# Block attention and a gated feed-forward layer in one kernel: signs of eight weight tiles, one scaling and a run of zero products move to other places

## The chip, the cores and the metric

The kernel runs on one core of one Trainium2 chip. The metric is device time in microseconds (us). Three runs of the kernel before took 1049.8, 1050.09 and 1050.73 us (median 1050.09).

## The reference, cut to what matters

```
scores = 0.125 * q @ k.T            # 8 batches, 8 heads, 576 positions, head size 64
scores = where(block_i >= block_j, scores, -1e9)      # blocks of 64 positions
attn   = exp(scores - rowmax);  attn /= rowsum + 1e-9
x = (attn @ v), heads side by side  # 4608 tokens x 512
h = x @ w_in                        # 512 x 2048, 64-bit floats
g = h * sigmoid(h)
out = g @ w_out                     # 2048 x 512, 64-bit floats
```

The two weight matrices arrive as 64-bit floats and are turned into 32-bit floats on the chip. Every product of the feed-forward layer and of the late attention is done with each 32-bit operand cut into a high part (a rounded copy, `fp32r`) and a low part (the rest).

## The kernel before, in words

The feed-forward layer works on 18 blocks of 256 tokens, each in 8 steps `d` over the 2048 inner columns (256 per step): `ffn1` (line 599, four 128x256 pieces in three products each, for two halves), then `silu` (L606), `g_hi` (L612), `g_lo` (L617) and, two steps later, `ffn2` (L629). One `ffn` in the order is half a step of either.

The tokens of the feed-forward blocks come from three kinds of attention. `First` (`a` and `b`) is the first block of 64 positions for all batches, in two groups; `a` yields block 0 of the feed-forward layer and `b` block 1. `Second` (`c0` to `c3`) is the second block of 64 positions. `Unit` (`u0` to `u63`) is one head of one batch for the other 448 positions. For `a`, `b` and `c` the steps are: `load` and `load_v` (DMA), `scores` (TensorE, L505 or L557), `max` and `sub` (VectorE, L433 and L436), `exp` (ScalarE, L439), `sum` (VectorE, L444 to L447), `norm` (the scaling by 1/sum, L450; on VectorE for `a` and `b`, on GpSimd for `c`), `turn` (transposes on TensorE, L457), `back` (ScalarE, L460), `pv` (TensorE, L519 or L575), `hi` (ScalarE, L524 or L580) and `lo` (VectorE, L528 or L583).

The weights come in 32 tiles `w0` to `w31` of 128x512 64-bit words: `w0`, `w1` belong to step 0 of `ffn1`, `w2`, `w3` to its step 1, `w4`, `w5` to step 0 of `ffn2`, `w6`, `w7` to step 2 of `ffn1`, and so on in turn. A tile is loaded (L187 or L190), the upper word scaled on ScalarE (`rebias`, L200), put together in three bit steps on VectorE (`bits:0`, `bits:1`, `bits:2`, L208, L212, L216; the first shifts and masks, the second adds the sign, the third adds the bits of the lower word), and cut into the high part (`hi`, ScalarE, L224) and the low part (`lo`, GpSimd, L227). Between `bits:0` and `bits:2` the half-made tile stands in a bank of PSUM.

The order of everything up to the 17th `Unit` is written out by hand in the string `ORDER`; a loop over the rest follows. Each engine runs its own instructions in that order and waits only for data and for free buffers. Loads all go through the queue of SyncE, in order. The buffers of `a`'s and `b`'s query and key tiles are used again by `w2` to `w5`, those of `b`'s scores (`T`) by `w7`.

Before the first real product TensorE multiplies 18 pairs of 64-column zero tiles (L415).

Of the kernel before, what the change touches and what calls it, by code (L numbers as in the profile page):

```python
# [55 lines left out]
a.lo:0 a.hi:1 b.pv w4.bits:0 w3.hi a.lo:1 w3.lo c0.load w4.bits:1 ffn w4.bits:2 b.hi:0 w7.load w2.lo b.hi:1 w5.bits:0 w8.load
w4.hi ffn w5.bits:1 w6.rebias w4.lo b.lo:0 ffn w5.bits:2 b.lo:1 w9.load w6.bits:0 c0.scores:0 silu w6.bits:1 g_hi ffn w6.bits:2
w7.rebias g_lo c0.max:0 w10.load w8.rebias ffn w7.bits:0 c0.load_v w5.hi w7.bits:1 silu w5.lo ffn c0.sub:0 w6.hi w7.bits:2 g_hi
w6.lo w8.bits:0 c0.scores:1 w9.rebias w11.load w7.hi w8.bits:1 ffn w10.rebias w8.bits:2 w7.lo w9.bits:0 w8.hi w12.load ffn g_lo
w9.bits:1 w9.bits:2 ffn w8.lo c0.max:1 w9.hi w13.load w10.bits:0 w11.rebias ffn w9.lo c0.sub:1 silu w10.bits:1 g_hi w10.bits:2 ffn  # L60
g_lo w11.bits:0 w14.load c0.exp w11.bits:1 ffn w11.bits:2 w12.rebias c0.sum w10.hi ffn w15.load w13.rebias w10.lo w12.bits:0 ffn
c0.norm w12.bits:1 silu w11.hi w12.bits:2 ffn w14.rebias w13.bits:0 w16.load w12.hi w11.lo w13.bits:1 c0.turn:0 c1.load g_hi ffn
w13.bits:2 c0.back:0 w12.lo w15.rebias w14.bits:0 w17.load c0.turn:1 w14.bits:1 g_lo ffn c0.back:1 w14.bits:2 w13.hi w15.bits:0
w16.rebias c0.pv w18.load w13.lo silu w15.bits:1 ffn w15.bits:2 c0.hi w16.bits:0 w14.hi w19.load g_hi ffn c0.lo w14.lo w17.rebias
w16.bits:1 w16.bits:2 c1.scores:0 g_lo w17.bits:0 w20.load ffn w17.bits:1 silu c1.max:0 w15.hi ffn c1.sub:0 w18.rebias w15.lo
w17.bits:2 g_hi w16.hi c1.scores:1 w18.bits:0 w21.load w17.hi g_lo w18.bits:1 w19.rebias ffn w18.bits:2 w16.lo w19.bits:0 ffn
w18.hi w22.load c1.max:1 w17.lo w20.rebias w19.bits:1 ffn silu w19.bits:2 w18.lo w20.bits:0 w19.hi w23.load ffn w20.bits:1
w21.rebias w19.lo g_hi c1.sub:1 ffn w20.bits:2 g_lo w21.bits:0 w24.load ffn w21.bits:1 c1.exp w21.bits:2 w20.hi ffn c1.sum
w22.rebias w25.load w20.lo w23.rebias c1.load_v ffn w22.bits:0 c2.load c1.norm w22.bits:1 silu ffn w22.bits:2 w24.rebias w21.hi
w23.bits:0 w26.load c1.turn:0 w23.bits:1 w21.lo ffn c1.back:0 w23.bits:2 g_hi w24.bits:0 w22.hi c1.turn:1 w27.load ffn w24.bits:1  # L70
w22.lo c1.back:1 w25.rebias w24.bits:2 w23.hi c1.pv g_lo w25.bits:0 w28.load w25.bits:1 w26.rebias ffn w23.lo c2.load_v c1.hi
w25.bits:2 w26.bits:0 ffn w29.load c1.lo w27.rebias w24.hi w26.bits:1 c2.scores:0 w25.hi w26.bits:2 w24.lo silu ffn w27.bits:0
w26.hi w30.load w25.lo w27.bits:1 g_hi w28.rebias ffn w27.bits:2 g_lo w29.rebias w28.bits:0 w31.load w27.hi ffn w28.bits:1 w26.lo
w28.bits:2 ffn w29.bits:0 w27.lo w30.rebias w29.bits:1 ffn w29.bits:2 w31.rebias w30.bits:0 silu ffn w30.bits:1 g_hi w30.bits:2
ffn g_lo w31.bits:0 c3.load c2.max:0 ffn c2.sub:0 silu w31.bits:1 w29.hi g_hi c2.scores:1 w31.bits:2 w28.hi ffn w28.lo c2.max:1
u0.load c2.sub:1 c3.scores:0 g_lo ffn mask c3.max:0 c2.exp c3.sub:0 w29.lo w31.hi c3.scores:1 c2.sum w30.hi w31.lo c3.load_v ffn
c3.max:1 c2.norm c3.sub:1 ffn c3.exp ffn w30.lo c3.sum c2.turn:0 silu ffn c2.back:0 c3.norm u0.split_hi c2.turn:1 ffn c2.back:1
g_hi c3.turn:0 g_lo c2.pv c3.back:0 c3.turn:1 u0.split_lo u0.load_v ffn c3.back:1 silu c3.pv g_hi ffn g_lo u1.load c3.hi c2.hi
c3.lo ffn c2.lo output silu u0.scores g_hi u0.v_hi g_lo ffn u0.max u1.split_hi ffn u1.split_lo u0.max2 ffn silu output ffn u0.v_lo
u2.load u0.sub ffn u1.load_v g_hi store g_lo u1.scores store u0.exp:0 ffn u1.max u2.split_hi u0.exp:1 ffn u2.split_lo u0.exp:2  # L80
u0.p_hi:0 u1.max2 ffn u0.p_hi:1 ffn u0.p_lo:0 u3.load silu u1.sub g_hi u0.p_lo:1 ffn u0.p_hi:2 u0.sums g_lo u2.scores u0.p_lo:2
silu ffn u2.max u3.split_hi u0.pv u3.split_lo u2.max2 u1.exp:0 ffn u1.exp:1 u1.exp:2 ffn u1.p_hi:0 u4.load g_hi u2.sub u1.p_lo:0
u1.p_hi:1 ffn u1.v_hi u1.p_lo:1 u0.lower u1.sums u1.p_hi:2 ffn g_lo u3.scores u0.fold u1.v_lo u2.exp:0 u1.sums2 u1.p_lo:2 ffn
u2.load_v u4.split_hi output ffn u3.max u4.split_lo output u2.exp:1 u1.pv u2.exp:2 u3.max2 ffn silu u5.load g_hi ffn u2.p_hi:0
g_lo u3.sub u1.lower u2.p_hi:1 ffn u2.p_lo:0 silu u1.fold u4.scores u2.p_lo:1 u2.sums g_hi u2.p_hi:2 u2.v_hi ffn u2.p_lo:2 u4.max
ffn u2.v_lo u3.exp:0 g_lo u1.mult u3.exp:1 ffn u3.load_v u5.split_hi u4.max2 u2.pv u3.exp:2 u5.split_lo ffn silu u4.sub u1.x_hi
ffn u2.lower u6.load u1.x_lo u3.p_hi:0 u3.sums ffn u3.p_hi:1 u3.p_hi:2 u3.p_lo:0 u3.v_hi u5.scores g_hi u2.fold u3.p_lo:1 u3.sums2
ffn g_lo u6.split_hi ffn u3.v_lo u5.max silu u3.p_lo:2 u4.load_v ffn u4.exp:0 u5.max2 u6.split_lo u4.exp:1 u3.pv g_hi u4.exp:2 ffn
u4.p_hi:0 u5.sub u3.lower g_lo u7.load u4.v_hi ffn u4.p_hi:1 u4.p_lo:0 u3.fold store u6.scores u4.sums u4.p_lo:1 silu ffn
u4.p_hi:2 u4.v_lo u6.max u7.split_hi ffn u4.p_lo:2 u5.load_v u3.mult ffn u7.split_lo u5.exp:0 u6.max2 u5.exp:1 u4.pv g_hi u5.exp:2  # L90
ffn g_lo u8.load u5.v_hi u6.sub u3.x_hi ffn store u4.lower u3.x_lo u5.p_hi:0 u5.sums ffn u5.p_lo:0 silu u7.scores u5.v_lo u4.fold
u5.p_hi:1 u5.p_hi:2 u5.sums2 u5.p_lo:1 u6.load_v ffn u5.p_lo:2 u6.exp:0 ffn u7.max u8.split_hi g_hi u5.pv u8.split_lo u6.exp:1
u6.exp:2 u7.max2 ffn u6.p_hi:0 u5.lower u6.v_hi ffn g_lo u9.load u6.p_hi:1 u7.sub ffn u6.p_lo:0 u5.fold u6.v_lo u8.scores silu
u6.sums u6.p_lo:1 g_hi u7.load_v u6.p_hi:2 ffn u9.split_hi g_lo u8.max ffn u6.p_lo:2 silu u5.mult ffn u9.split_lo u8.max2 u7.exp:0
u6.pv u7.exp:1 g_hi u7.exp:2 ffn g_lo u7.p_hi:0 u10.load u8.sub u5.x_hi ffn u6.lower u5.x_lo u7.p_hi:1 u7.sums u7.p_hi:2 ffn
# [710 lines left out]
```

## Time and profile before

| what | value |
|---|---|
| time of the profiled execution | 1050.03 us |
| its span, first to last instruction | 1048.3 us |
| median of three runs | 1050.09 us |
| TensorE busy | 1027.9 us, 98% |
| VectorE busy | 767.1 us, 73% |
| ScalarE busy | 750.5 us, 72% |
| GpSimd busy | 741.4 us, 71% |

The page names the engines PE (TensorE), DVE (VectorE), ACT (ScalarE), POOL (GpSimd) and SP (SyncE). The shares are means over a span that has a start, a stretch in which weights are made, a long steady stretch and an end with only the feed-forward layer; what one stretch waits for is read from its own rows. A record of the profile for a 32-bit float product is half of one, so 18 zero products have 36 records.

### The profile page before, as it was taken

What the parts mean: (1) busy time and instruction counts of PE and PEld (TensorE: products, weight loads), DVE (VectorE), ACT (ScalarE), POOL (GpSimd) and SP (SyncE); (2) the same over time, 40 slices, a digit from 0 to 9 for tenths busy, and PEclk for the clock granted to TensorE, in tenths of its full rate; (3) what the DMA queues carried; (4) which work ended last, traced back from release to release, by engine and by line L of the source; (5) the groups of instructions that cost most, each with busy time, mean ns of one, the idle gap of its engine ahead of it and who ended that gap; (6) DMA issues with size and microseconds to landing.
All of it is one profiled execution on the core that took longest, in us unless ns stands there. A gap on an engine that the chain in (4) does not pass through costs nothing.

```text
span 1048.3 us, 19893 instructions
## 1 busy us (share of the span) xinstructions
PE 1027.9 (98%) x6996; PEld 931.2 (89%) x6996; DVE 767.1 (73%) x2238; ACT 750.5 (72%) x1195; POOL 741.4 (71%) x721
## 2 busy tenths in 40 slices
PE   5999999999999999999999999999999999999998
PEld 4888898888899999999999999998999999989987
DVE  7998499999968888888888887888888888700000
ACT  4876578898987778787878787878788877722222
POOL 1676679888886878787878787878787878622221
PEclk6999999999999999999999999999999999999999
DMA  6777223223223222222222223222222222000000
GB/s 245 248 236 247 58 73 84 70 74 79 65 53 91 54 53 74 54 73 54 74 54 74 59 61 81 56 78 53 73 54 74 54 73 53 18 11 21 1 21 21
DMA packets 35043, 79.93 MB, mean 76 GB/s; under 512 B 4736, under 2 KB 12928, under 8 KB 34944
## 3 DMA queue, kind: packets, MB, share of 16 engines
q1 hardware_dynamic: 34944, 78.66, 26.8%
q8 instruction: 56, 0.92, 0.4%
...
## 4 chain that ended last, share of the span: by engine, by line
PE 82%; DVE 7%; ACT 4%; POOL 3%; issue 2%; DMA 2%; SPq 0%; DVEq 0%; ACTq 0%; POOLq 0%
PE o L629 33%; PE h L599 33%; PE S L289 7%; PE U L368 7%; DVE wm L216 1%; DVE Dx L233 1%; DVE S L212 1%; DMA qkraw<-in_qk_dram 1%; DVE S L208 1%; DVE Mx L233 1%; POOL pl L344 1%; DMA wst<-in_moe_w_in_dram 1%; ACT p L330 1%; PE S L629 1%; ACT g L606 0%
## 5 line engine op out<-in xcount | busy, mean ns | idle before, releaser
L599 PE MATMUL h<-x,wi 128*128 128x256 f32 x3456 | 440.6, 281 | 0.3 <-POOL x L405 0.3
L599 PEld LDWEIGHTS h<-x,wi 128*128 128x128 f32 x3456 | 429.9, 188 | 11.8 <-issue 0.5
L629 PE MATMUL o<-wo,g 128*128 128x512 f32 x1680 | 424.7, 398 | 0.0
L629 PEld LDWEIGHTS o<-wo,g 128*128 128x128 f32 x1680 | 305.8, 188 | 62.6 <-issue 0.3
L344 POOL TENSOR_TENSOR pl<-p,ph 128x448 fp32r<-128x448 f32 (+1 forms) x192 | 226.0, 1201 | 95.2 <-ACT ph L336 95.2
L617 POOL TENSOR_TENSOR g<-g,g 128x512 fp32r<-128x512 f32 x144 | 186.3, 1294 | 122.1 <-ACT g L612 117.1
L233 DVE TRANSPOSE_TENSOR_REDUCE Mx<-S 64x4 f32<-64x128 f32 (+4 forms) x384 | 135.6, 405 | 99.2 <-PE S L289 98.8
L606 ACT ACTIVATE g<-h 128x512 f32<-128x512 f32 x144 | 86.1, 598 | 124.6 <-POOL g L617 75.3
L612 ACT CAST g<-g 128x512 fp32r<-128x512 f32 x144 | 89.2, 619 | 60.8 <-PE o L629 59.0
L233 DVE TRANSPOSE_TENSOR_REDUCE Dx<-p 128x14 f32<-128x448 f32 (+3 forms) x320 | 122.8, 446 | 0.2
L330 ACT ACTIVATE p<-T 128x512 f32<-128x512 f32 (+1 forms) x192 | 105.6, 604 | 12.5 <-POOL ph L346 11.8
L336 ACT CAST ph<-p 128x512 fp32r<-128x512 f32 (+1 forms) x192 | 104.5, 595 | 0.3 <-PE U L368 0.2
L265 POOL TENSOR_TENSOR qh<-qkraw,qh 64x576 fp32r<-64x576 f32 x64 | 91.5, 1430 | 15.3 <-ACT qh L261 10.7
L289 PE MATMUL S<-qh 128*128 128x448 f32 (+3 forms) x320 | 91.1, 298 | 0.0
L606 ACT ACT_TABLE_LOAD x67 | 86.0, 1283 | 1.2
L289 PE MATMUL S<-ql,qh 128*128 128x448 f32 (+3 forms) x320 | 84.0, 307 | 0.0
L330 ACT ACT_TABLE_LOAD x63 | 80.8, 1283 | 1.5
L267 POOL TENSOR_TENSOR ql<-qkraw,qh 128x448 fp32r<-128x448 f32 x64 | 74.1, 1158 | 5.0
L368 PE MATMUL U<-ph,vc 128*128 128x448 f32 (+3 forms) x320 | 74.4, 297 | 1.8 <-DVE xu L384 1.3
L321 DVE TENSOR_TENSOR T<-S,MR 128x256 f32<-128x256 f32 (+2 forms) x192 | 73.1, 407 | 0.0
L261 ACT CAST qh<-qkraw 128x1024 fp32r<-128x1024 f32 x64 | 66.9, 1045 | 6.7 <-DMA qkraw<-in_qk_dram 5.4
L276 POOL TENSOR_TENSOR vc<-vraw,vc 128x320 fp32r<-128x320 f32 x64 | 56.6, 884 | 13.9 <-ACT vc L273 13.4
...
## 6 DMA issues: line engine op xcount, KB each, us to landing
qkraw<-in_qk_dram SPq DMA_DIRECT2D x128, 256.0 KB, 4.0
...
```

What stands on the lines that cost most here:

```text
L233: nc.vector.tensor_reduce(out=out, in_=in_, axis=AX.X, op=op, apply_transpose=True)
L265: nc.gpsimd.tensor_tensor(out=u.qh[64:, NQ:], in0=u.raw[64:, NQ:], in1=u.qh[64:, NQ:], op=ALU.subtract)
L289: nc.tensor.matmul(u.ps(c, w, m), u.kk[:, j * P : j * P + m], qq[:, q0 : q0 + w], start=i == 0, stop=i == 1)
L330: nc.scalar.activation(u.p[:, c:e], T[:, c:e], AF.Exp, scale=SCALE)
L336: nc.scalar.copy(u.ph[:, c:e], u.p[:, c:e])
L344: nc.gpsimd.tensor_tensor(out=u.pl[:, c:e], in0=u.p[:, c:e], in1=u.ph[:, c:e], op=ALU.subtract)
L368: nc.tensor.matmul(U[:m, q0 : q0 + w], u.vc[:, j, :m], (u.ph, u.pl)[pp][:, c : c + w], start=n == 0, stop=n == 8)
L599: nc.tensor.matmul(h[:, f, :], wi[wt][:, c, w], x[:, xt, :], start=n == 0, stop=n == 3 * CT - 1)
L606: nc.scalar.activation(g, hs.pop((blk, d)), AF.Silu)
L612: nc.scalar.copy(g2[:, 0], g)
L617: nc.gpsimd.tensor_tensor(out=g2[:, 1], in0=g, in1=g2[:, 0], op=ALU.subtract)
L629: nc.tensor.matmul(o, g2[:, gt, f, tk], wo[wt][:, 2 * d + f, :], start=d == 0 and n == 0, stop=d == NSTEP - 1 and n == 5,)
```

## The change

It has three parts and a new order.

1. For `w0` to `w7` a new step `sign` on GpSimd multiplies the upper word of the 64-bit float, read as a 32-bit float, by zero: the result is +0 or -0. It is written into the place where the low part will stand later. For these tiles `bits:0` shifts and ORs that signed zero in at once, and `bits:1` is not issued. The other 24 tiles keep three steps.
2. `norm` of `b` is issued on GpSimd instead of VectorE.
3. The zero products become a step `warm` of 18 products that the order calls: once at the start, as before, and three times in a row behind the scores of `b`, ahead of the first `turn`.

In the new order the loads of `a` and `b` stand ahead of those of the weights, and the steps up to the 17th `Unit` are placed anew.

```
-w0.load a.load w1.load b.load w0.rebias w0.bits:0 w0.bits:1 w0.bits:2 a.scores w1.rebias w1.bits:0 w2.load a.max:1 a.max:0
+warm a.load b.load w0.load w1.load a.scores a.max:1 w2.load b.scores warm warm warm a.max:0 a.sub:0 w0.rebias w0.sign a.sub:1
+b.max:0 w4.load w1.sign w3.load b.max:1 b.load_v w0.bits:0 a.exp b.sub:0 w2.sign a.load_v b.sub:1 w1.rebias a.sum b.exp w5.load
...
+        def sign(u):
+
+            u.zeros = u.parts[1]
+            nc.gpsimd.tensor_scalar(out=u.zeros, in0=u.shaped(u.word(1).bitcast(F32)), scalar1=0.0, scalar2=None, op0=ALU.mult)
+
         def bits(u, j):
...
             if j == 0:
                 u.a = bank(1).bitcast(U32)
+            if j == 0 and u.zeros is not None:
+                nc.vector.scalar_tensor_tensor(
+                    out=u.shaped(u.a), in0=u.shaped(w), scalar=3, in1=u.zeros.bitcast(U32), op0=ALU.logical_shift_left, op1=ALU.bitwise_or
+                )
+            elif j == 0:
...
-    for i in range(WARM):
-        nc.tensor.matmul(idle[:64, :64], zero, zero, start=True, stop=True)
+
+    def warm():
+        for i in range(WARM):
+            nc.tensor.matmul(idle[:64, :64], zero, zero, start=True, stop=True)
...
-        KEYS, engine = 64, nc.vector
+        KEYS = 64
 
         def __init__(u, g):
-            u.g, u.m, u.lane = g, {}, 0
+            u.g, u.m, u.lane, u.engine = g, {}, 0, (nc.vector, nc.gpsimd)[g]
```

On VectorE, from its first step on, this stood in the order before (L208, L212 and L216 are the bit steps, `m` the row maxima, `p` the scores of `a` and `T` those of `b`):

```order
L208 TENSOR_SCALAR S_126<-wm 128x512
L212 SCALAR_TENSOR_TENSOR S_126<-wst,S_126 128x512
L216 SCALAR_TENSOR_TENSOR wm<-wst,S_126 128x512
L208 TENSOR_SCALAR S_167<-wm 128x512
L433 TENSOR_REDUCE m<-U_131 128x8
L433 TENSOR_REDUCE m<-S_130 128x8
L212 SCALAR_TENSOR_TENSOR S_167<-wst,S_167 128x512
L436 TENSOR_TENSOR p_132<-S_130,m 128x8x64
L436 TENSOR_TENSOR p_132<-U_131,m 128x8x64
L216 SCALAR_TENSOR_TENSOR wm<-wst,S_167 128x512
L433 TENSOR_REDUCE m<-o 128x8 x2
```

and this stands there now (L215 is the new first bit step with the signed zero `wi_74`, L227 the last one, L457 to L463 the sum and the scaling):

```order
L446 TENSOR_REDUCE m<-U_125 128x8
L446 TENSOR_REDUCE m<-S_124 128x8
L449 TENSOR_TENSOR p_126<-S_124,m 128x8x64
L449 TENSOR_TENSOR p_126<-U_125,m 128x8x64
L446 TENSOR_REDUCE m<-o 128x8 x2
L215 SCALAR_TENSOR_TENSOR S_271<-wm,wi_74 128x512
L449 TENSOR_TENSOR T<-o,m 128x8x64 x2
L457 TENSOR_REDUCE U_125<-p_126 128x16
L458 TENSOR_SCALAR U_125<-U_125 128x16
L460 RECIPROCAL rr<-U_125 128x16
L463 TENSOR_TENSOR p_126<-p_126,rr 128x1024
L457 TENSOR_REDUCE o<-T 128x16
```

The bit steps of `w0` and `w1` have moved from ahead of `a`'s maxima and between its steps to one step ahead of `b`'s subtraction and the rest behind `b`'s sum.

On GpSimd, from the making of the identity matrix on, this stood in the order before (L227 is `lo` of a weight tile):

```order
L419 AFFINE_SELECT ident<-ident 128x128
L227 TENSOR_TENSOR wi_74<-wm,wi_73 128x2x256 x2
L227 TENSOR_TENSOR wi_74<-MR,wi_73 128x2x256 x2
L227 TENSOR_TENSOR wo_76<-wm,wo_75 128x512
L617 TENSOR_TENSOR g_434<-g,g_434 128x512
```

and this stands there now (L206 is `sign`, L463 with `T` the scaling of `b`, L238 `lo`):

```order
L432 AFFINE_SELECT ident<-ident 128x128
L206 TENSOR_SCALAR wi_74<-wst 128x2x256 x4
L206 TENSOR_SCALAR wo_76<-wst 128x512
L463 TENSOR_TENSOR T<-T,rr 128x1024
L238 TENSOR_TENSOR wi_74<-wm,wi_73 128x2x256 x2
L206 TENSOR_SCALAR wo_76<-wst 128x512
L238 TENSOR_TENSOR wi_74<-MR,wi_73 128x2x256 x2
L206 TENSOR_SCALAR wi_74<-wst 128x2x256
L238 TENSOR_TENSOR wo_76<-wm,wo_75 128x512
L206 TENSOR_SCALAR wi_74<-T 128x2x256
```

Five signs and the scaling of `b` stand ahead of the first `lo`, three more signs between the next ones.

On TensorE, behind the scores of `b`, this stands now (L428 are the zero products, L470 the two halves of `a`'s `turn`):

```order
L518 MATMUL o<-qk_116 64x64 x16
L518 MATMUL o<-qk_117 64x64 x16
L428 MATMUL S_88<-zero 64x64 x54
L470 MATMUL U_125<-ident,p_126 128x128 x4
L470 MATMUL S_124<-ident,p_126 128x128 x4
```

The row of 54 is new; the other four stood there in the same sequence.

## Rows read from the trace of the kernel before

**Rows 1.** The page: span, then the chain that ended last, by engine.

```profile
span 1048.3 us, 19893 instructions
...
PE 82%; DVE 7%; ACT 4%; POOL 3%; issue 2%; DMA 2%; SPq 0%; DVEq 0%; ACTq 0%; POOLq 0%
```

**Rows 2.** Busy time by stretch (stretch, length, then each engine's busy time and count).

```profile
0.00:28.10 28.10, 14.89 (x308) 13.06 (x308) 19.77 (x32) 12.33 (x19) 3.62 (x12) 0.70 0.71 250
28.10:130.00 101.90, 100.18 (x827) 88.34 (x822) 82.49 (x139) 71.81 (x114) 69.99 (x57) 1.00 0.62 195
130.00:275.00 145.00, 143.23 (x925) 129.94 (x924) 136.49 (x430) 125.44 (x198) 124.92 (x121) 1.00 0.30 75
275.00:908.00 633.00, 632.72 (x4084) 577.32 (x4083) 521.58 (x1621) 502.20 (x801) 506.88 (x503) 1.00 0.24 63
```

**Rows 3.** TensorE's timeline of the start (start, length, instructions, [idle before, releaser]).

```profile
1.06 4.10 PE L415 MATMUL S<-zero 128*64 128x64 f32 x36 [1.06 <-DVE zero L412]
6.07 0.27 PE L505 MATMUL S<-qk 64*64 64x64 f32 x1 [0.91 <-DMA qk<-in_qk_dram]
...
10.32 1.13 PE L505 MATMUL o<-qk 64*64 64x64 f32 x32 [1.91 <-DMA qk<-in_qk_dram]
11.62 1.13 PE L505 MATMUL o<-qk 64*64 64x64 f32 x32 [0.17 <-DMA qk<-in_qk_dram]
19.87 1.08 PE L457 MATMUL U<-ident,p 128*128 128x128 f32 x4 [7.11 <-DVE p L450]
...
24.40 1.95 PE L457 MATMUL o<-ident,T 128*128 128x128 f32 x8
...
27.03 1.15 PE L519 MATMUL o<-T,v 64*64 64x64 f32 x62 [0.42 <-ACT T L460]
28.12 4.50 PE L599 MATMUL h<-x,wi 128*128 128x256 f32 x36
```

**Rows 4.** TensorE in three half microseconds (busy, then granted clock, DMA share, GB/s).

```profile
8.50:9.00 0.50, 0.00 (x0) 1.00 1.00 397
9.50:10.00 0.50, 0.00 (x0) 0.50 0.94 385
26.50:27.00 0.50, 0.11 (x2) 1.00 0.85 311
```

**Rows 5.** ScalarE's timeline of the start.

```profile
4.76 0.66 ACT L200 ACTIVATE wm<-wst 128x512 f32<-128x512 f32 x1 [2.67 <-DMA wst<-in_moe_w_in_dram]
...
13.42 1.06 ACT L439 ACTIVATE p<-p 128x1024 f32<-128x1024 f32 x1 [3.74 <-DVE p L436]
...
14.93 1.12 ACT L224 CAST wi<-wm 128x512 fp32r<-128x512 f32 x2
...
21.04 0.58 ACT L460 COPY p<-U 128x512 f32<-128x512 f32 x1 [3.58 <-PE U L457]
```

**Rows 6.** VectorE's timeline of the start.

```profile
13.90 1.28 DVE L433 TENSOR_REDUCE m<-o 128x8 f32<-128x512 f32 x2
...
16.29 1.22 DVE L444 TENSOR_REDUCE U<-p 128x16 f32<-128x1024 f32 x1
...
17.76 0.26 DVE L447 RECIPROCAL rr<-U 128x16 f32<-128x16 f32 x1
...
18.52 1.21 DVE L450 TENSOR_TENSOR p<-p,rr 128x1024 f32<-128x1024 f32 x1
...
32.75 0.68 DVE L208 TENSOR_SCALAR S<-wm 128x512 uint32<-128x512 uint32 x1
33.47 0.70 DVE L212 SCALAR_TENSOR_TENSOR S<-wst,S 128x512 uint32<-128x512 uint32 x1
```

**Rows 7.** GpSimd's timeline: the one-input operation, `lo`, and the scaling of `c0`.

```profile
1.47 0.29 POOL L419 TENSOR_SCALAR_AFFINE_SELECT ident<-ident 128x128 f32<-128x128 f32 x1
...
30.59 1.29 POOL L227 TENSOR_TENSOR wo<-wm,wo 128x512 fp32r<-128x512 f32 x1
...
49.82 1.90 POOL L450 TENSOR_TENSOR MR<-MR,rr 128x1024 f32<-128x1024 f32 x1
```

More of the change, by code (lines that the diff above doesn't have):

```diff
@@ L56 @@
[L56 to L95, printed above, removed]
@@ L116 @@
-u16.p_lo:0 u16.v_hi ffn u16.p_hi:2 u16.p_lo:1 ffn u16.p_lo:2 silu u15.lower g_hi u16.v_lo g_lo u17.load_v store
+warm a.load b.load w0.load w1.load a.scores a.max:1 w2.load b.scores warm warm warm a.max:0 a.sub:0 w0.rebias w0.sign a.sub:1
+b.max:0 w4.load w1.sign w3.load b.max:1 b.load_v w0.bits:0 a.exp b.sub:0 w2.sign a.load_v b.sub:1 w1.rebias a.sum b.exp w5.load
+w2.rebias a.norm w3.sign b.sum a.turn:1 w4.sign a.turn:0 a.back:1 a.back:0 w0.bits:2 b.norm a.pv w1.bits:0 w0.hi w3.rebias
+w1.bits:2 w2.bits:0 w0.lo w1.hi b.turn:1 w6.load a.hi:0 w2.bits:2 b.turn:0 b.back:1 w1.lo a.lo:0 b.back:0 w3.bits:0 a.hi:1 b.pv
@@ new lines @@
+w5.sign w2.hi a.lo:1 w5.rebias w3.bits:2 w4.rebias w2.lo ffn w3.hi w4.bits:0 w7.load b.hi:0 w4.bits:2 w3.lo w6.rebias ffn
+w5.bits:0 b.hi:1 w8.load w4.hi w6.sign w5.bits:2 c0.load ffn b.lo:1 w9.load w4.lo b.lo:0 ffn w6.bits:0 silu w7.sign w6.bits:2
+w7.rebias w5.hi ffn w10.load w8.rebias w5.lo w7.bits:0 g_hi ffn w7.bits:2 g_lo w8.bits:0 w7.hi w11.load c0.scores:0 w8.bits:1
+w7.lo w8.bits:2 w9.rebias ffn w6.hi c0.max:0 w12.load w8.hi w9.bits:0 w6.lo c0.load_v ffn silu c0.sub:0 g_hi w9.bits:1 w8.lo
@@ new lines @@
+g_hi ffn c0.back:0 w16.bits:2 g_lo w17.bits:0 c0.turn:1 w20.load ffn w15.lo w17.bits:1 c0.back:1 w18.rebias w17.bits:2 w16.hi
+c0.pv w18.bits:0 w21.load silu w16.lo w18.bits:1 w19.rebias ffn c0.hi w18.bits:2 w17.hi c0.lo ffn w22.load w20.rebias w17.lo
+w19.bits:0 g_hi c1.load_v w18.hi w19.bits:1 c1.scores:0 g_lo w19.bits:2 ffn w20.bits:0 w23.load w18.lo c1.max:0 silu ffn c1.sub:0
+g_hi w20.bits:1 w21.rebias g_lo w20.bits:2 c1.scores:1 w22.rebias w19.hi w21.bits:0 w24.load w20.hi ffn w21.bits:1 w20.lo
@@ new lines @@
+w21.bits:2 ffn silu w22.bits:0 w25.load w19.lo c1.max:1 w21.hi ffn c1.sub:1 w21.lo w23.rebias w22.bits:1 w24.rebias ffn w22.bits:2
+g_hi w23.bits:0 w26.load g_lo ffn w23.bits:1 c1.exp w23.bits:2 ffn w24.bits:0 w22.hi w27.load c1.sum w25.rebias w22.lo ffn
+w24.bits:1 silu c1.norm ffn w24.bits:2 w26.rebias g_hi w25.bits:0 w28.load ffn w23.hi w25.bits:1 w24.hi w23.lo w25.bits:2
+c1.turn:0 w26.bits:0 ffn w29.load w24.lo c1.back:0 w26.bits:1 c2.load w27.rebias w26.bits:2 w25.hi c1.turn:1 g_lo ffn w27.bits:0
@@ new lines @@
+c1.back:1 w30.load w26.hi w27.bits:1 w25.lo w28.rebias c1.pv w27.bits:2 w26.lo w28.bits:0 ffn c1.hi c2.load_v w28.bits:1 silu
+w28.bits:2 ffn w29.rebias w31.load c1.lo w27.hi w29.bits:0 g_hi w27.lo c2.scores:0 w30.rebias w29.bits:1 w29.bits:2 ffn g_lo
+w30.bits:0 ffn w30.bits:1 w31.rebias w30.bits:2 silu c2.max:0 ffn c3.load g_hi w31.bits:0 c2.sub:0 g_lo ffn w31.bits:1 w31.bits:2
+c2.scores:1 silu mask w28.hi ffn c2.max:1 u0.load w31.hi w30.hi c2.sub:1 w31.lo c3.scores:0 w29.hi ffn w28.lo c3.max:0 c2.exp
```

83 lines of the change are left out of this document (53 added, 30 removed).

## The prediction, made before the changed kernel had run

> **What bounds the kernel now.** I read the page first, for the span and for the chain that ended last: 82% of it is TensorE, 7% VectorE, 4% ScalarE [rows 1]. Where the rest of it lies is read by stretch [rows 2]. In the first 28.1 us TensorE is busy for 14.89. From 28.1 to 130 it lacks 1.7 us, from 130 to 275 another 1.8, and from 275 to 908 it is busy for 632.72 of 633.00. So from 28 us on the time is TensorE's own work, the same in both kernels, and two things can be gained: an earlier first product of the feed-forward layer (28.12 [rows 3]) and some of the 3.5 us of idle time between 28 and 275.
>
> Third I read the start on TensorE [rows 3]. Zero products run until 5.16, the scores of `a` begin as their tiles land, those of `b` at 10.32, and then TensorE waits 7.11 us for VectorE's scaling of `a`. From 19.87 it turns, multiplies and turns again until 28.12. The clock stands beside it [rows 4]: 1.00 at 8.5, 0.50 at 9.5 after scores with gaps between them, 1.00 again at 26.5, behind the turning of `b`. So the first turning and most of what follows it ran at 1.2 GHz: eight transposes 1.95 us [rows 3].
>
> Last I read what VectorE does before 19.87. The scaling of `a` (18.52) follows the sum of `a` (16.29), which follows bit steps of `w0` and `w1` and the maxima of `b` [rows 6]; ScalarE's exponent of `a` waits 3.74 us for VectorE and starts at 13.42 [rows 5].
>
> **The change, part by part.** The sum is made against the profiled execution's own 1050.03 us (span 1048.3 and 1.7 around it); the median of the runs is 1050.09, so nothing is to be added.
>
> *Loads.* The first transfer has landed at 4.76 [rows 5]; the two tiles of `b` land 1.30 apart (10.32 and 11.62, [rows 3]). In the new order: tiles of `a` 4.8 and 6.1, of `b` 7.4 and 8.7, then `w0` 10.0, `w1` 11.3, `w2` 12.6, `w4` 13.9, `w3` 15.2, values of `b` 16.5, of `a` 17.8. The loads of `w2` and `w4` wait in SyncE's queue for the scores of `a` and `b`, whose buffers they take, and hold those behind them; at 9.8 the transfers of `w0` and `w1` still run, so nothing lands later for it. The values of `a` are first wanted at about 19.6, below.
>
> *VectorE to the first turning.* The scores of `b` end at 8.7 + 1.13 = 9.8 at the lower clock. Two maxima take 1.28 (to 11.1). `w0.bits:0` needs `rebias` (10.0 + 0.66) and `sign`. The trace has no GpSimd product with a constant. From below: the only other one-input operation, 0.29 us for 128 columns [rows 7], as if its size cost nothing. From above: `lo`, 1.29 with two inputs. I take 0.9, nearer to 0.29 times a size of four (1.16) than to 0.29. With 0.9 the sign ends at 10.9, hidden by the maxima of `b`; with 1.29 the path grows by 0.2. Then `w0.bits:0`, two subtractions (starts 0.6 apart, from the 1.28 for two), the sum of `a` at 12.85, its reciprocal 1.47 later, the scaling from 14.6 to 15.8 (1.21) [rows 6]. The first turning could start at 15.9 instead of 19.87.
>
> *Zero products.* They stand in front of it: 54, so 108 records. The row of 36 took 4.10, 0.114 each [rows 3]. All at that rate: 12.3 us; all at half of it (the upper clock): 6.2. From 9.8 they end between 16.0 and 22.1. I take 36 records at the slow rate, as in the row after which the scores of `a` ran at the upper level, and 72 at the fast one: 4.1 + 4.1 = 8.2, end 18.0. So they, not VectorE, release the turning, 1.9 us earlier than before.
>
> *From the turning to the first feed-forward product.* At the upper clock the eight transposes take half of 1.95, 0.98. Then ScalarE leads, in its order: second `back` of `a` 0.58, `w0.hi` 0.56, `w3.rebias` 0.66, `w1.hi` 0.56, `a.hi:0` 0.58, two `back` of `b` 1.16, `a.hi:1` 0.58 [rows 5] (`hi` of `a` is a copy of the same size), and VectorE's `a.lo:1` 0.68. That is 6.3, so 24.3. Beside it lie the product with `a`'s values (from 19.6; 1.15, as `b`'s [rows 3]), `b`'s turning and `b`'s product (22.9 to 24.1). `b`'s scaling goes to GpSimd, 1.90 instead of 1.21 [rows 6, 7]: its sum is ready at about 17.4, five signs in front of it end by 17.1, so it ends at 19.3, before `b`'s turning at 20.7, and costs nothing; VectorE is free of 1.21. First product at 24.4 instead of 28.12: 3.7 us.
>
> *Weights afterwards.* Eight `bits:1` go, 0.72 from start to start [rows 6]: 5.8 us off VectorE, 7.0 with the scaling, more than the 3.7 by which TensorE wants the tiles earlier. GpSimd gets 8 x 0.9 + 1.9 = 9.1 us; it is busy for 3.62 in the first 28.1 [rows 2], so they fit, with `w5` to `w7`'s signs between the first `lo`s. If that cover is gone, each sign puts off a `lo` by 0.9. With VectorE ahead, part of the 3.5 us of idle time should go; a new order can also open other gaps. I count 0.6.
>
> Sum: 1050.03 - 3.7 - 0.6 = 1045.7.
>
> **A rule that speaks against it.** Before, every bit step reads one operand from SBUF and one from PSUM, or one alone; the new `bits:0` reads two from SBUF, while GpSimd reads there too. The trace has no row of VectorE with two SBUF operands beside a busy GpSimd; both scalings of VectorE (1.21) run while GpSimd rests. The Trainium skill, "SBUF — State Buffer", section "Who interferes with whom", says that such a VectorE instruction and a GpSimd one that reads SBUF share a read interface, and that the later one is held until the earlier is done. No row here shows it or denies it; it is the second rival.
>
> **Rivals.**
> - *Zero products mostly at the upper clock, or the gaps close.* They end at 16.0; then VectorE leads: `b`'s sum, then four bit steps, to 19.55; `w1.hi` to 20.1, then 0.58 + 1.16 + 0.58 + 0.68 gives 23.1, 5.0 us gained; with 1.3 of idle time back: 1043.7. For it: the scores of `a` end later and with smaller gaps than before. Against: the clock fell after such scores [rows 4].
> - *VectorE and GpSimd hold each other.* `w1.bits:0`, ready at 18.1, waits for `b`'s scaling until 19.3. Then six VectorE steps of 0.72 up to `w3.bits:0`, two waits of half a `lo` (1.3 together) and `a.lo:1` 0.68: 25.6, 2.5 us gained, and nothing of the idle time: 1047.5. By that rule, this.
> - *The new order opens gaps later.* TensorE idles for another 3.5 us between 25 and 275, as much as now [rows 2], behind the weights or the steps of `c`: 1045.7 + 0.6 + 3.5 = 1049.8. For it: every step there is placed anew, and VectorE is busy for 136 of 145 us in that stretch. Against: VectorE has 7 us less to do.
> - *Slower: the zero products hold the turning.* All 108 at 0.114 end at 22.1. At the upper clock the path behind is 6.4, first product 28.5: 1050.4. If the clock stays low behind them as well, the path is the one of before, 28.12 - 19.87 = 8.25, first product 30.4: 1052.3. It decides from an end of the zero products after 21.7 on. Against: after 36 such products scores ran fast.
>
> **How the numbers follow.** The forecast 1045.7 gets 0.50, with its own range 1044.3 to 1047.0 (end of the zero products 16.5 to 19.5, idle time back 0 to 1.3). The faster rival gets 0.16, the held engines 0.18, gaps later 0.09, slower 0.07. A measurement tells a change from about 0.2%, 2.1 us: faster means below 1048.0. The forecast and the first rival lie there, and two thirds of the second (0.12): 0.78. Same: the rest of it, most of the gaps and the milder end of the last (0.06 + 0.08 + 0.02): 0.16. Slower: 0.06. The range of 8 in 10 runs from 1043.2 to 1048.8.
>
> **What would show it.** Right: zero products in one unbroken row from about 9.8 to 18, the clock rising inside it; the first turning straight behind them, eight transposes in about 1 us; first feed-forward product at 24 to 25; TensorE's idle time from there to 275 below 3.5 us; sign rows of 0.6 to 1.2 us. Wrong: zero products beyond 21.7; new first bit steps much longer than 0.70 or waiting beside GpSimd's rows; a first product before 25 with a gain under 2 us, which would put the loss into the stretch from 25 to 275.

## The result: slower by 0.4%, and the loss falls at one place

The changed kernel took 1054.28 us (median of six runs, 1053.62 to 1055.13), the kernel before beside it 1050.16 (1049.8 to 1050.73): a ratio of 1.0039, 95% interval 1.0026 to 1.0052. The forecast was 1045.7. The profiled execution has a span of 1052.3 us against 1048.3 [rows 1].

The busy time of the changed kernel by stretch (columns as in [rows 2]):

```profile
0.00:28.10 28.10, 21.18 (x425) 19.67 (x426) 19.87 (x27) 13.79 (x22) 17.21 (x20) 0.88 0.69 249
28.10:130.00 101.90, 97.97 (x806) 85.81 (x805) 79.96 (x129) 69.34 (x110) 70.82 (x57) 1.00 0.63 195
130.00:275.00 145.00, 144.32 (x931) 130.85 (x930) 137.08 (x431) 123.65 (x197) 126.76 (x124) 1.00 0.30 74
275.00:908.00 633.00, 630.10 (x4066) 575.20 (x4065) 518.86 (x1616) 500.07 (x795) 503.14 (x498) 1.00 0.25 63
```

The last of them is the row to look at first: TensorE, busy for 632.72 of 633 us before [rows 2], lacks 2.90. Where time is gained or lost is seen best by counting TensorE's feed-forward products (`h<-x,wi`) in both traces and subtracting the start times of equal numbers. The 1st starts 2.07 us earlier than before, the 49th 2.33 earlier, the 961st, at 321, 0.31 earlier, the 1009th, at 340, 4.03 later, and from there to the last the difference stays between 3.9 and 4.05. Between the 49th and the 961st the difference goes up and down by one or two microseconds (0.29 later at the 97th, 1.17 later at the 481st), in part because the two orders put other products between these. So of a lead of two microseconds 0.3 is left at 321, and the loss falls between 321 and 340.

There, TensorE's timeline in the kernel before (first row) and in the changed kernel:

```profile
321.37 3.18 PE L599 MATMUL h<-x,wi 128*128 128x256 f32 x24
```

```profile
321.06 1.48 PE L612 MATMUL h<-x,wi 128*128 128x256 f32 x10
325.14 3.33 PE L612 MATMUL h<-x,wi 128*128 128x256 f32 x14 [2.60 <-POOL x L416]
```

and two stretches of it (TensorE's busy time first, its granted clock third from the right):

```profile
321.00:324.00 3.00, 1.54 (x12) 1.24 (x10) 2.76 (x9) 2.93 (x8) 2.92 (x3) 1.00 0.00 0
324.00:330.00 6.00, 4.86 (x21) 4.56 (x22) 0.00 (x0) 5.37 (x9) 6.00 (x8) 0.72 0.49 117
```

The row of 24 products stops after ten and waits 2.60 us for the low part of its tokens (`x_lo`, L416) from GpSimd. Behind the wait the granted clock is 0.72 on average over six us, so for part of them it was at 1.2 GHz: the other fourteen products took 3.33 us. All 24 from the same place took 3.18 in the kernel before and 3.17 in e1_load_first below, 0.132 each; the fourteen would have been 1.85, so the clock cost 1.5 there. Followed back, first GpSimd's timeline and then ScalarE's:

```profile
320.95 1.44 POOL L276 TENSOR_TENSOR qh<-qkraw,qh 64x576 fp32r<-64x576 f32 x1 [5.24 <-ACT qh L272]
...
324.78 1.43 POOL L416 TENSOR_TENSOR x<-xu,x 128x64 fp32r<-128x64 f32 x3
```

```profile
319.76 1.05 ACT L272 CAST qh<-qkraw 128x1024 fp32r<-128x1024 f32 x1 [6.25 <-DMA qkraw<-in_qk_dram]
```

GpSimd stands 5.24 us for ScalarE, ScalarE 6.25 us for the load of the next unit's queries and keys. And the queue of loads (SyncE; the length of a grouped row reaches from its first issue to its last):

```profile
301.54 0.33 SPq L268 DMA_DIRECT2D vraw<-in_v_dram  x1
301.92 1.11 SPq L655 DMA_DIRECT2D out_dram<-ot  x2
314.48 0.33 SPq L268 DMA_DIRECT2D vraw<-in_v_dram  x1
314.86 9.87 SPq L264 DMA_DIRECT2D qkraw<-in_qk_dram  x4
```

Values have one buffer. The values of unit 17 can be asked for only when GpSimd has cut those of unit 16 (`vc`, 313.58 to 314.45). In the new `ORDER` the load of unit 18's queries and keys (`u18.load`) is the very last word, behind `u17.load_v`; SyncE takes its queue in order, so it stood there with a free buffer and went out at 314.86. In the kernel before it stood 25 words from the end and went out at 304.81:

```profile
304.81 1.11 SPq L253 DMA_DIRECT2D qkraw<-in_qk_dram  x2
```

Nothing of this has to do with signs, scalings or zero products.

The start, on TensorE, answers to [rows 3]:

```profile
9.13 6.51 PE L428 MATMUL S<-zero 128*64 128x64 f32 x108
16.41 0.63 PE L470 MATMUL U<-ident,p 128*128 128x128 f32 x4 [0.76 <-DVE p L463]
...
18.78 0.24 PE L532 MATMUL S<-p,v 64*64 64x64 f32 x1 [1.31 <-DMA v<-in_v_dram]
...
21.48 1.97 PE L470 MATMUL o<-ident,T 128*128 128x128 f32 x8 [1.47 <-POOL T L463]
24.13 1.99 PE L532 MATMUL o<-T,v 64*64 64x64 f32 x64 [0.68 <-ACT T L473]
26.05 7.12 PE L612 MATMUL h<-x,wi 128*128 128x256 f32 x50
```

The zero products end at 15.64, so it is VectorE's scaling of `a` (until 16.26) that releases the first turning. That runs at the upper clock (0.63 instead of 1.08 for four), and then come three waits, for `a`'s values, for GpSimd's scaling and for ScalarE's copies. Two half microseconds show the clock: granted 0.50 at 22.0, and 1.00 again at 28.5:

```profile
22.00:22.50 0.50, 0.50 (x4) 0.50 (x3) 0.48 (x1) 0.00 (x0) 0.50 (x1) 0.50 0.93 336
...
28.50:29.00 0.50, 0.50 (x6) 0.50 (x5) 0.40 (x2) 0.08 (x1) 0.50 (x1) 1.00 0.99 385
```

So `b`'s turning takes 1.97 as before the change, and the first products run at half rate. GpSimd's signs (L206) and its scaling (L463), and VectorE's new first step (L215), which answers to the last two of [rows 6]:

```profile
9.91 1.53 POOL L206 TENSOR_SCALAR wi<-wst 128x512 fp32r<-128x512 f32 x1 [8.16 <-DMA wst<-in_moe_w_in_dram]
...
18.04 1.52 POOL L206 TENSOR_SCALAR wo<-wst 128x512 fp32r<-128x512 f32 x1
19.52 1.91 POOL L463 TENSOR_TENSOR T<-T,rr 128x1024 f32<-128x1024 f32 x1
21.38 2.96 POOL L238 TENSOR_TENSOR wi<-wm,wi 128x512 fp32r<-128x512 f32 x2
24.32 1.98 POOL L206 TENSOR_SCALAR wo<-wst 128x512 fp32r<-128x512 f32 x1
...
31.16 1.29 POOL L238 TENSOR_TENSOR wo<-wm,wo 128x512 fp32r<-128x512 f32 x1
```

```profile
11.47 0.70 DVE L215 SCALAR_TENSOR_TENSOR S<-wm,wi 128x512 uint32<-128x512 uint32 x1 [0.93 <-ACT p L452]
...
18.56 0.70 DVE L215 SCALAR_TENSOR_TENSOR S<-wm,wi 128x512 uint32<-128x512 uint32 x1
...
20.11 1.88 DVE L215 SCALAR_TENSOR_TENSOR S<-MR,wi 128x512 uint32<-128x512 uint32 x1
...
23.23 1.67 DVE L215 SCALAR_TENSOR_TENSOR S<-MR,wi 128x512 uint32<-128x512 uint32 x1
...
31.65 1.36 DVE L215 SCALAR_TENSOR_TENSOR S<-wm,wi 128x512 uint32<-128x512 uint32 x1
```

The same VectorE instruction takes between 0.70 and 1.88. The eight add up to 10.7 us; in the three-step form these tiles would take sixteen steps of 0.69 to 0.70, 11.1. A sign takes 1.53, and 1.98 where it begins while such a step runs; two `lo` take 2.96 instead of 2.5.

What beside GpSimd makes a step long can be read from the starts. Six of the eight begin inside a GpSimd row with two inputs (`lo` or the scaling), and each of the six ends 0.56 after that row: the step at 31.65 ends at 33.01, the `lo` at 32.45. The step at 18.56 lies wholly inside a sign (18.04 to 19.56) and takes 0.70, as the one at 11.47 does with GpSimd at rest.

### The profile page after: what moved, and what is told of

The parts are those of the page before. It is cut to its first block, busy times and chain, and to the rows that moved or that the text cites. A ratio compares the mean times of both kernels' runs of the same rounds, so it can differ in the third digit from the quotient of the medians.

```text
span 1052.3 us, 20112 instructions
## 1 busy us (share of the span) xinstructions
PE 1034.4 (98%) x7104; PEld 937.6 (89%) x7104; DVE 766.5 (73%) x2229; ACT 748.6 (71%) x1193; POOL 757.3 (72%) x730
## 4 chain that ended last, share of the span: by engine, by line
PE 86%; DVE 7%; DMA 2%; ACT 2%; POOL 2%; issue 1%; SPq 0%; DVEq 0%; ACTq 0%; POOLq 0%
PE o L642 34%; PE h L612 34%; PE S L300 8%; PE U L379 8%; DVE wm L227 1%; DVE S L223 1%; DVE S L219 1%; DMA wst<-in_moe_w_in_dram 1%; DVE Dx L244 1%; DVE Mx L244 1%; DMA wst<-in_moe_w_out_dram 1%; DMA qk<-in_qk_dram 1%; PE S L642 0%; POOL wi L206 0%; PE S L570 0%
## 5 line engine op out<-in xcount | busy, mean ns | idle before, releaser
L619 ACT ACTIVATE g<-h 128x512 f32<-128x512 f32 x144 | 86.1, 598 | 121.7 <-POOL g L630 77.2
L272 ACT CAST qh<-qkraw 128x1024 fp32r<-128x1024 f32 x64 | 66.9, 1045 | 15.6 <-DMA qkraw<-in_qk_dram 11.3
```

The source lines that it names most:

```text
L619: nc.scalar.activation(g, hs.pop((blk, d)), AF.Silu)
```

## The experiments

Every run stood beside runs of the kernel before on its chip. These gave medians of 1050.41 (e1 to e4), 1050.72 (e5 to e8; e9 to e11) and 1050.44 us (e12).

**e1_load_first**: the changed kernel, two words of `ORDER` exchanged.

```
-g_lo u17.load_v u18.load
+g_lo u18.load u17.load_v
```

> The changed kernel with one difference: in the last row of ORDER the load of attention unit 18's queries and keys (u18.load) stands ahead of u17.load_v instead of behind it. In the trace of the changed kernel SyncE waits at u17.load_v until 314.48 us, until GpSimd has let go of the one buffer for values, and only then issues u18.load; its data land at 319.7, ScalarE stands 6.25 us at the split of these data, GpSimd's x_lo behind it is 2.6 us late, TensorE stands 2.60 us at 322.5 and then runs 3.4 us at the lower clock level. Theory Q (the queue order of two loads makes the whole loss): the load is issued ahead of 310 us, no wait over 0.5 us stands at 322, the time falls by 2.6 + 1.7 = 4.3 to 1050.0 (1049.4 to 1050.6), 0.3 under the kernel before at most. Rival R (the wait moves to another instruction of the same chain, because the finer order around 300 to 320 is late as a whole): the wait at 322 stays over 1.5 us and the time at 1052.5 to 1054.5.

Measured: 1050.15 us, ratio to the kernel before 0.9996 (0.9987 to 1.0005). The load goes out 8 us earlier, ScalarE's split of it waits for TensorE's scores only, and the wait at 322 is gone:

```profile
306.86 1.13 SPq L264 DMA_DIRECT2D qkraw<-in_qk_dram  x2
314.06 0.33 SPq L268 DMA_DIRECT2D vraw<-in_v_dram  x1
```

```profile
320.61 3.17 PE L612 MATMUL h<-x,wi 128*128 128x256 f32 x24
```

**e2_before_load_last**: the kernel before, with the load where the changed kernel has it.

```
-... u16.load_v ffn u18.load u15.p_lo:2 ...
+... u16.load_v ffn u15.p_lo:2 ...
-... u17.load_v store
+... u17.load_v u18.load store
```

> The kernel before with one difference: u18.load moved from two thirds of the last-but-one row of ORDER to behind u17.load_v, where the changed kernel has it. Theory Q: it is issued at about 315.1 instead of 304.8 us, ScalarE's split of it begins at about 319.5 instead of 314.6, x_lo of GpSimd comes 2 to 2.5 us later, TensorE stands 2 to 2.6 us there and then loses 1 to 1.7 us to the lower clock level: 1050.1 + 3 to 4.3 = 1053.1 to 1054.4. Rival R (the load's place matters only together with the rest of the new order): within 0.7 of the kernel before, 1049.8 to 1050.8.

Measured: 1054.42 us, ratio 1.0037 (1.0024 to 1.0049). The same chain, and the same wait to the hundredth:

```profile
320.48 1.05 ACT L261 CAST qh<-qkraw 128x1024 fp32r<-128x1024 f32 x1 [5.80 <-DMA qkraw<-in_qk_dram]
```

```profile
325.85 1.91 PE L599 MATMUL h<-x,wi 128*128 128x256 f32 x14 [2.60 <-POOL x L405]
```

Taken out of the changed kernel it takes the loss away; put into the kernel before it makes the loss. Theory Q is shown both ways, R falls. One part of the expectation missed: in this profiled execution the clock stayed at 1.00 behind the wait and the fourteen products took 1.91. By that execution, the fastest of the five with 1053.29 us, the place cost 2.9; the median is 1.1 higher, which would fit executions with the lower clock, but only the profiled one shows its clock there.

What remains is why a lead of 2.3 us at the start is worth nothing. The next ten runs are about that.

**e3_norm_on_vector**: e1 with `b`'s scaling on VectorE.

```
-... u.engine = g, {}, 0, (nc.vector, nc.gpsimd)[g]
+... u.engine = g, {}, 0, nc.vector
```

> e1_load_first with the scaling of block b by VectorE again (First.engine = nc.vector for both blocks). In the changed kernel TensorE waits 1.47 us ahead of b's turning for GpSimd's scaling, which ran from 19.52 to 21.43 behind three signs, and its clock falls to the lower level from 21.4 to 28.2. Theory N (the scaling on GpSimd is on the path of the first feed-forward product): VectorE scales at 17.9 to 19.1, b's turning begins 1.5 to 2 us earlier, the first feed-forward product at 24.3 to 25.2 instead of 26.05, and the time is 0.8 to 2 us below that of e1_load_first. Rival V (VectorE's 1.22 us more push the bit steps of the first weights back, and these end last): first product at 25.7 to 26.8 and the time within 0.6 of e1_load_first.

Measured: 1049.6 us, ratio 0.9992 (0.9983 to 1.0001). Theory N missed: `b`'s turning began at 20.32 at the upper clock (1.09), but ScalarE's copies of it stand behind `w1.hi`, that behind VectorE, and there the first step of `w1` took 1.78 beside GpSimd's `lo` of `w0`; TensorE waited 3.43, and the first feed-forward product came at 26.76. The wait went elsewhere; V's numbers fit.

**e4_no_signs**: e1 with three bit steps for all tiles and no signs on GpSimd; for each of `w0` to `w7`, as here:

```
-... w0.rebias w0.sign a.sub:1
+... w0.rebias a.sub:1
-... w0.bits:0 a.exp ...
+... w0.bits:0 w0.bits:1 a.exp ...
```

> e1_load_first without the signs by GpSimd: all eight tiles take the three bit steps of the kernel before on VectorE (bits:1 put right behind bits:0). In the changed kernel the eight two-step tiles' first step takes 0.70 to 1.88 us on VectorE, 10.7 us in all, against 16 steps of 0.69 = 11.1 in the three-step form; GpSimd's signs take 1.53 to 1.98 us each, 13 to 14 us in all, and its lo steps beside them 1.48 to 1.5 instead of 1.29. Theory P (the two engines hold one another at memory, so the signs save VectorE nothing and load GpSimd): b's scaling on GpSimd starts when its sums are there, at about 18 instead of 19.5, the first feed-forward product comes 0.3 to 1.5 us earlier or at the same time and the time is 0 to 1.5 us below e1_load_first. Rival S (the signs do save VectorE 0.69 us each on the path): first product 0.7 to 1.5 us later, the time 0.7 to 2.5 us above e1_load_first.

Measured: 1049.13 us, ratio 0.9988 (0.998 to 0.9997): as theory P has it, first product at 24.48. Here the 108 zero records took 8.01 us, to 17.97, and held the turning by 1.1: the rival in which they all run slowly, in small.

**e5_no_zeros**: e1 without the zero products ahead of the turning.

```
-... b.scores warm warm warm a.max:0 ...
+... b.scores a.max:0 ...
```

> e1_load_first without the three times 36 records of zero products ahead of the first turning. With them the first turning ran at the upper clock level (0.63 us for its first four instead of 1.08 in the kernel before) but the level fell again at about 21.4 us, as TensorE had waited for the value loads and for GpSimd's scaling, and the first feed-forward products ran at the lower level until 28.2. Theory Z0 (the zeros bring nothing that lasts): first feed-forward product at 25.4 to 26.4, the time within 0.7 of e1_load_first's 1050.15. Rival Z1 (what they gain at the turning and at the first products stays): the first products later by 1 us or more and the time 0.8 to 2 us above e1_load_first.

Measured: 1049.91 us, ratio 0.9994 (0.9985 to 1.0003). The turning ran at the lower clock again (1.09), the first product came at 25.06. Z0: in this order the zeros bring nothing that can be measured.

**e6_no_signs_one_warm**: e4 with one `warm` instead of three.

```
-... b.scores warm warm warm a.max:0 ...
+... b.scores warm a.max:0 ...
```

> e4_no_signs with one group of zero products (18 products, 36 records) ahead of the first turning instead of three. In e4_no_signs the 108 records took 9.96 to 17.97 and TensorE reached the turning after VectorE's scaling was done (it ended at 16.85), so the zeros held the turning by 1.05. Theory H (the hold is what they cost there): the turning begins at 16.9 to 17.1, the first feed-forward product at 24.0 to 24.6, the two waits of TensorE for VectorE's x (1.7) come as before since VectorE's own rows set them, and the time is within 0.5 of e4_no_signs' 1049.13. Rival K (the shorter stretch loses the upper clock level and with it turning, products with v and the first feed-forward products take longer): first feed-forward product at 25 or later, the time 0.7 to 2 us above e4_no_signs.

Measured: 1049.3 us, ratio 0.9986 (0.9977 to 0.9995). The time is H's, the profiled start K's (turning at 18.30 and at 1.08, first product at 26.5). Inconclusive: the profiled execution took 1050.4, 1.1 more than the median, and its first load of a weight tile landed at 11.95 instead of 10.64 in e4, so its late start says little of the others.

**e7_signs_unused**: e1 with the signs written and not used; lo writes over them.

```
-u.zeros = u.parts[1]
-nc.gpsimd.tensor_scalar(out=u.zeros, ...)
+nc.gpsimd.tensor_scalar(out=u.parts[1], ...)
```

> e1_load_first with GpSimd's eight signs written but not used: VectorE makes the three bit steps of the kernel before for these tiles (as in e4_no_signs), GpSimd still writes the signs, and lo writes over them. Theory P2 (VectorE and GpSimd hold one another only where VectorE's step takes two operands from SBUF, as the two-step form's first step does; the three-step form has one in PSUM): VectorE's three steps stay at 0.69 each, none of the first 24 over 0.75, and GpSimd's signs at 1.53 without the long ones of 1.98. The time is 0 to 1.2 above e4_no_signs since b's scaling stands behind signs again: 1049.1 to 1050.4. Rival P3 (any work of GpSimd slows VectorE's steps, whatever their operands): steps of 1 us and more in the first 30 us, first feed-forward product 26.5 or later, the time over 1050.8.

Measured: 1049.19 us, ratio 0.9986 (0.9978 to 0.9995). VectorE's steps from 8 to 32 us, and GpSimd's signs of the input weights (least, median and greatest length in ns):

```profile
L222 DVE SCALAR_TENSOR_TENSOR S<-wst,S 128x512 uint32<-128x512 uint32 x6 | 4.2, 696 | 0.2
```

```profile
L205 POOL TENSOR_SCALAR wi<-wst x5: 1527/1537/2355, 11.8 to 29.8; 128x512 fp32r<-128x512 f32 x5
```

With the same signs on GpSimd, VectorE's steps stay at 0.69 once none has two operands in SBUF. P2 holds, P3 falls. The one long sign (2.36) began at 16.99 while VectorE scaled `a` (from 16.72), which reads two operands from SBUF. Three steps without signs (e4) and with unused ones (e7) have the same median, so the signs by themselves cost nothing that can be measured.

**e8_before_zeros**: the kernel before with the zeros alone (`warm` made a function as in the change).

```
-w1.bits:1 b.scores a.sub:0 ...
+w1.bits:1 b.scores warm warm warm a.sub:0 ...
```

> The kernel before with the change's three times 36 records of zero products behind b's scores, and nothing else. In the kernel before TensorE is idle from 12.8 to 19.87 there, its first turning runs at the lower clock level (1.08 us for four) and its first feed-forward product starts at 28.12. Theory Z0 (zeros ahead of the turning do little, as waits follow): turning shorter by 0.9 in all, first feed-forward product at 27.2 to 28.2, the time within 0.8 below the kernel before, 1049.3 to 1050.4. Rival Z2 (zeros at the lower level last longer than the idle time and hold the turning): they end after 20.5, the time 0.5 to 2 us above the kernel before.

Measured: 1049.76 us, ratio 0.9989 (0.9981 to 0.9998), the first product at 26.25, 0.95 earlier than Z0 expected. Z2 falls. With nothing else changed the zeros gain one microsecond (1.0 by the medians, 0.9 at the last product), and keep it; in e5 the same zeros brought nothing.

By now a pattern stood in the traces. VectorE's last bit step, in the kernel before and in the changed one:

```profile
100.74 0.69 DVE L216 SCALAR_TENSOR_TENSOR wm<-T,S 128x512 uint32<-128x512 uint32 x1
```

```profile
101.64 0.69 DVE L227 SCALAR_TENSOR_TENSOR wm<-T,S 128x512 uint32<-128x512 uint32 x1
```

Its start, set beside those of the first and the 481st feed-forward product (the profiled execution of each kernel, us from the span's start):

```
kernel         first product   last bit step   481st product   difference of the last two
before             28.12          100.74          167.75          67.0
changed            26.05          101.64          168.92          67.3
e1                 25.54          101.21          168.46          67.3
e4                 24.48          100.23          167.36          67.1
e5                 25.06          101.67          168.95          67.3
e7                 25.73          103.25          170.51          67.3
e8                 26.25           99.67          166.78          67.1
e11 (below)        29.24          103.39          170.77          67.4
e12 (below)        26.75           99.91          167.15          67.2
```

The last column hardly moves, while the first one tells little: e7's first product is earlier than e8's and its 481st is 3.7 later. (In e2, e3, e9 and e10 the difference is 67.1, 66.8, 67.3 and 66.9, in e6 68.0.) The rows belong to one execution each, not to the median: e7's was the slowest of its runs, and the kernel before, e2 and e11, which are the same up to the first product, have it at 28.12, 28.43 and 29.24. The next two runs test whether VectorE's chain is the cause.

**e9_before_zeros_norm**: e8 with `b`'s scaling on GpSimd.

```
-KEYS, engine = 64, nc.vector
...
+... u.engine = g, {}, 0, (nc.vector, nc.gpsimd)[g]
```

> e8_before_zeros with block b's scaling by GpSimd, as in the changed kernel, and no signs. In the eight profiles so far the moment at which VectorE ends its last bit step (99.67 to 103.25 us, 100.74 in the kernel before) and the start of the 481st feed-forward product agree within 0.5 us of one another's differences. Theory D (VectorE's chain of bit steps paces everything up to 101 us, whatever TensorE gains at the start): b's scaling takes 1.22 us off VectorE, its last bit step ends at 98.3 to 99.2 instead of 99.67 and the time falls by 0.5 to 1.3 below e8_before_zeros' 1049.76. Rival W (GpSimd's scaling takes 1.9 instead of 1.2 and b's turning waits for it): VectorE's last bit step at 99.6 or later and the time within 0.5 of 1049.76 or above.

Measured: 1050.64 us, ratio 0.9999 (0.999 to 1.0008); last bit step at 100.50. W, though not for its reason: TensorE waited only 0.3 for the scaling. Up to its last bit step VectorE works 0.7 us less than in e8 (86.1 and 86.8) but stands idle 1.6 longer (14.4 and 12.9), in four waits of 0.2 to 0.6 that e8 does not have, the longest for ScalarE's rebias of a tile. Work taken off VectorE is worth something only if its next tile is there.

**e11_three_more_steps**: the kernel before with VectorE's first bit step of three tiles made twice.

```
-nc.vector.tensor_scalar(out=u.a, in0=w, ...)
+for _ in range(1 + (u in wts[8:11])):
+    nc.vector.tensor_scalar(out=u.a, in0=w, ...)
```

> The kernel before with VectorE's first bit step of tiles w8, w9 and w10 made twice: three more instructions of 0.69 us, 2.08 us in all, with the same result. Theory D (VectorE paces the stretch up to 101 us): its last bit step ends 1.9 to 2.2 us later than 100.74, and the time rises by 1.5 to 2.2 to 1052 to 1052.8. Rival T (TensorE, or the loads, pace it and VectorE has slack): the time rises by less than 0.7.

Measured: 1053.12 us, ratio 1.0019 (1.001 to 1.0028), so 2.0 us for 2.08 of work (2.4 by the medians); last bit step at 103.39, 2.65 later than in the kernel before, more than D's 1.9 to 2.2. Part of that is the execution: its first product, ahead of the added steps, is 1.1 later already. VectorE has no slack there: theory D, and T falls.

**e10_rebias_to_psum**: e1 with ScalarE's rebias of the eight tiles written to PSUM, so that the new first step has one operand in SBUF; the rebiases of `w2`, `w3` and `w5` move behind the last step of the tile two before.

```
-nc.scalar.activation(u.w, u.word(1).bitcast(F32), AF.Copy, scale=REBIAS)
+if k < 8:
+    u.a = bank(1 + k % 2).bitcast(U32)
+nc.scalar.activation(u.w if u.a is None else u.a.bitcast(F32), ...)
...
-out=u.shaped(u.a), in0=u.shaped(w), scalar=3, in1=u.zeros ...
+out=u.shaped(u.a), in0=u.shaped(u.a), scalar=3, in1=u.zeros ...
```

> e1_load_first with one difference for the eight tiles with signs: ScalarE writes the rebiased words to PSUM (two banks in turn, so that w2 to w7 are rebiased only behind the second step of the tile two before), and VectorE's first step reads them there and works in place, with the signs as its only operand in SBUF. Theory H (VectorE and GpSimd hold one another where a VectorE step has two operands in SBUF): the first step takes 0.66 to 0.78 us each time instead of 0.70 to 1.88, GpSimd's signs 1.53 but for one beside the scaling of block a, VectorE's eight steps 5.6 instead of 10.7. Theory D on top of it (VectorE paces the stretch up to 101 us): its last bit step ends 2.5 to 5 us earlier than 101.2, at 96.2 to 98.7, and the time is 1045 to 1047.7. Rival B (the banks make ScalarE and VectorE wait for one another, or TensorE is the limit there anyway): steps of 0.7 but VectorE idle in their place, time 1049 to 1051.

Measured: 1048.87 us, ratio 0.9981 (0.997 to 0.9993). The first step of the input weights (least, median, greatest):

```profile
L218 DVE SCALAR_TENSOR_TENSOR S<-S,wi x6: 685/692/699, 13.3 to 35.2; 128x512 uint32<-128x512 uint32 x6
```

Theory H is shown: 0.69 us each beside the same signs, `lo` and scaling of GpSimd. The time is between the two: the bank that w1's rebias takes belonged to the zero products, ScalarE stood 4.53 for them, and the last bit step came at 101.48.

**e12_rebias_own_bank**: e10 without that wait.

```
-idle = bank(2)
+idle = pH.tile([P, 2, TB], F32, tag="h", name="h")[:, 0]
...
-... a.hi:1 b.pv w5.sign ...
+... a.hi:1 w4.rebias b.pv w5.sign ...
-... w3.bits:2 w5.rebias w4.rebias ...
+... w3.bits:2 w5.rebias ...
```

> e10_rebias_to_psum with two waits of its own taken away: the zero products write to a bank of the feed-forward result, not to the bank that w1's rebias takes (in e10 ScalarE stood 4.53 us for that until 17.83, and block b's exponentials behind it), and the rebiases of w4 and w5 stand where their bank has just come free. Theory D with H (the two-step form without a second operand in SBUF saves VectorE 5 us, and VectorE paces the stretch up to 101): its last bit step ends at 96.5 to 99, the time is 1045.5 to 1048. Rival B (something else paces there once VectorE's steps are short: the loads, ScalarE's queue, TensorE): VectorE's last step at 99.5 or later, the time 1048 to 1050.

Measured: 1048.32 us, ratio 0.9976 (0.9965 to 0.9986), the fastest of all and faster than both kernels; last bit step at 99.91, so B's numbers. The eight first steps take 5.5 us, 4.1 less than in e1 (9.6), and of that about 1.3 arrive at the end of the chain (101.21 in e1): up to its last bit step VectorE stands idle for 18.6 us, in e1 for 15.8. From 28 to 102 us ScalarE's rebiases wait for their loads, 11.3 us in all in this trace (7.8 in e1, 6.3 before). That something paces the chain beside VectorE's own steps is shown; that it is the loads is a reading of those waits, and was not tested. The loads wait in turn, for 50.6 us of the first 102, until VectorE's last step of an earlier tile frees a buffer, so it may be the whole ring and not one engine.

## Why the prediction was wrong

**The step that failed** is the first one: "So from 28 us on the time is TensorE's own work, the same in both kernels", with all that can change put between 28 and 275. The row it rested on [rows 2] is right for the kernel before, but `ORDER` reaches to 322, and I did not look at its end, where the order of two loads in one queue had changed. That place measures +4.3 (the 961st to the 1009th product), 2.60 of it the wait and 1.5 the clock behind it, and e1 and e2 give 4.5 (1.0039 less 0.9996) and 3.9 for it. The rival of later gaps named the kind, at 0.09, but sought it before 275 and behind weights or steps of `c`, and counted no clock behind it.

**The first product at 24.4** came at 26.05. The turning itself came 1.6 earlier than forecast: the zeros took 6.51, near the low bound of 6.2, and VectorE, not they, released it, as the first rival has it. Behind it the terms were short: `a`'s values made TensorE wait 1.31; `b`'s scaling, "costs nothing", ended at 21.43 instead of 19.3 and made it wait 1.47; and the clock fell back, which the sum did not have (1.97 and 1.99 for turning and product where e4 shows 1.09 and 1.16: 1.7 us).

**The sign** was mis-sized: 0.9 taken, bounds 0.29 and 1.29, measured 1.53, outside both. With one input it takes longer than the two-input `lo` (1.29), which writes the same rounded type; whether it is slow because it reads every second word was not tried.

**"7.0 us off VectorE"** was the costliest error behind the place at 322. The new first step takes 10.7 instead of the 5.6 that the sum implied, so the bit steps give 0.4, and the last one ends 0.9 later than before. The reason is the one of the second rival, at 0.18: VectorE and GpSimd hold one another where a VectorE step has two operands in SBUF (e7 and e10). The Trainium skill, "SBUF — State Buffer", section "Who interferes with whom", says that a VectorE instruction with two SBUF inputs contends with a GpSimd one that reads SBUF, by an exclusive lock. The trace agrees for GpSimd's rows with two inputs: the step that begins at 20.11 meets the scaling (19.52 to 21.43) and ends at 21.99, 0.56 behind it, though a step takes 0.70 alone, so it was held to nearly the end. It does not agree for a sign that runs already, though that reads SBUF too: as far as the profile's times of GpSimd go, the step at 18.56 was not held at all (in e3 one that began at 24.75, 0.03 behind a sign, took 1.16). So it was `lo` and the scaling that held VectorE, and the signs that were held by it. The rival's own 1047.5 was wrong as well, as it did not have the place at 322.

**The lead was priced on the wrong engine.** I priced what the change brings at TensorE's first feed-forward product. From there to 101 us VectorE's chain has no slack (e11: 2.0 us for 2.08), so a gain there is worth what it moves VectorE's last bit step: 0.5 later in e1, 1.1 earlier in e8. Up to that step VectorE works 86.3 us and stands idle for 15.3 in the changed kernel, 86.9 and 13.9 in the kernel before: the work fell by 0.6, not by 7.0, and the idle time rose. Given back between 130 and 275, as forecast, were 1.1 us (0.68 of idle time instead of 1.77), against 2.2 more of it between 28 and 130 (3.93 and 1.72).
